# Block-sparse attention and a gated feed-forward layer on one core: half of the head-splitting copies change engine, and the attention stage is ordered anew

## The chip, the core and the metric

The kernel runs on one core of a Trainium2 chip. A core has five engines with instruction queues of their own: PE (TensorE, matmuls and transposes into PSUM; PEld is its loading of weights), DVE (VectorE), ACT (ScalarE), POOL (GpSimd) and SP (SyncE, which here only issues DMAs). Each engine works through its queue in order, and an instruction that waits holds up all that stand behind it on that engine. The metric is the device time of one execution in microseconds (us). Here 1% is 2.1 us.

## The reference

Attention over 4 batches, 8 heads, 768 positions and 64 columns per head, with a mask by blocks of 32 positions: a block sees its neighbours, the first and the last block, and three sampled blocks; the first and the last block see all. The result, as 3072 tokens of 512 columns, goes through a feed-forward layer with 1024 columns inside.

```python
scores = scale * np.matmul(q, k.transpose(0, 1, 3, 2))
mask = |blk_i - blk_j| <= 1, or first or last block in i or j, or kb in sampled_blocks[qb]
scores = np.where(mask, scores, -1e9)
attn = softmax(scores) @ v                 # -> x, (3072, 512)
h = x @ w_in                               # (3072, 1024)
solu = h * softmax(h)
ln = (solu - mean(solu)) / np.sqrt(var(solu) + 1e-6) * g_ln
out = ln @ w_out                           # (3072, 512)
```

## The kernel before, in words

**Layout.** Heads are taken in pairs (`pr`, 0 to 3). For a pair, K and Q are needed with the head's columns on the partitions: `kT` and `qT` hold, per pair, six chunks of 128 positions for each of two heads, on 64 + 24 partitions. The 24 are mask rows, so that one matmul over 88 partitions gives score plus mask; no mask is applied elsewhere. There are two buffers of each, for even and odd batches. `va` holds V with a column of ones, which gives the softmax's sum.

**Batch 0** is transposed by PE: `opening(pr)` casts a staged pair to bf16 (`cast`, L269), turns it on PE into a PSUM bank (`turned`, L463), and copies the bank to `kT` or `qT` (`evac`). The first pair comes in pieces, so that the first scores can begin early: K's first two chunks, then its other four in one piece of eight transposes and one evacuation.

**Batches 1 to 3** are transposed by the DMA crossbar. `crossed(b, pr, nm)` casts a loaded pair to bf16 (`kb`, `qb`), a DMA transposes it (`cross_kq`, issued by SP, into `kc` or `qx`), and there the two heads lie on partitions 0 to 63 and 64 to 127. Two copies named `split` part them: each moves 64 x 768 bf16 values of one head (`hh`) to partitions 0 to 63 of `kT` or `qT`. For `hh` = 1 the source starts at partition 64. There are 3 batches x 4 pairs x 2 tensors x 2 heads = 48 of them.

**Attention** is cut into 3 query tiles `t` of 256 positions. `attend(b, t, pr)` makes three groups of scores (L550, four matmuls each, into one of two PSUM tiles `s`), an exp of each on ACT (L556, 128 x 1024), then 24 matmuls with V (`pv`, L571, into one of two banks `mbank`), a reciprocal and a multiplication (`recip` L580, `norm` L583) into `x`.

**Feed-forward.** For each query tile `x` is transposed (`turn_x`: on PE for the first and the last tile, with `xevac` copies; by DMA otherwise), and each half of 128 tokens (`feed`, j = 0 to 23) runs: x @ w_in (L630, four 512-column matmuls per half of the 1024 columns), exp with sum (`silu_e`, L650, ACT), the product (`mult`, L653, DVE), two `stats` and an `aggr` (L660, L663, DVE), then `z2`, `vr` and `rs` (L666, L669, L702, POOL) for the factor of the row, a transpose of the product, ln @ w_out (L747), `scale` from PSUM to `ots` (L757 on DVE or L755 on ACT) and the store. `scale` frees the `mbank` of its output.

**Weights.** w_in is loaded in four pieces and cast (`wcast`); w_out in two. From w_out and the layer norm's factors VectorE sums rows (`wacc`, L422 and L424) and then makes the eight scaled and centred rows `wo` (L438, two SBUF inputs each); the first output projection needs them.

**Order.** The program is a list of operations. Each call of `op` appends one; `ORDER` gives the order of issue of all of them by their number in that list, and `ENGINES` puts some of them on another engine than the one in their `op` call. What is on one engine runs there in the order of `ORDER`. Buffers come from small pools (`take`, `last_of`), also in that order. A handful of `SPARES`, matmuls whose results nobody reads, stand in the list too.

Of the kernel before, what the change touches and what calls it, by code (L numbers as in the profile page):

```python
# [11 lines left out]
ACT = mybir.ActivationFunctionType  # L12
# [6 lines left out]
    "POOL": [7],  # L19
    "ACT": [9, 24, 127, 383, 543, 811, 1070, 1072, 1114, 1121],  # L20
    "DVE": [90, 92, 126, 134, 135, 154, 411, 622, 639, 653, 657, 863, 867, 872, 876, 886, 1116],
}
ORDER = [
# [112 lines left out]
def kernel(  # L136
# [21 lines left out]
    NPR = H // 2  # L158
# [22 lines left out]
    kT = bufs("kT", [P, NPR, NCH, 2, P], BF16, 2)  # L181
    qT = bufs("qT", [P, NPR, NCH, 2, P], BF16, 2)
# [6 lines left out]
    kc = bufs("kc", [P, NCH, 2, KR], BF16, NKC)  # L189
# [101 lines left out]
    kheld = [own1] + kown[1:]  # L291
# [152 lines left out]
    cover, kdone, qdone, mask1 = [], [], [], {}  # L444
# [409 lines left out]
```

## Time and profile before

| | |
|---|---|
| runs shown | 205.54, 206.61, 206.93 us; median 206.61 |
| profiled execution | 206.22 us, its span 204.2 us |
| granted TensorE clock | 1.000 |
| engines' busy time | PE 197.5, ACT 174.3, DVE 149.4, POOL 66.5 us |
| DMA | 43.17 MB, mean 211 GB/s |

The span runs from the first to the last instruction; 2.0 us lie around it. Lines like "L550" are lines of the kernel. Most copies and casts go through one helper, so they all have line 269 (267 on ACT) and are told apart by what they write and read: `kT<-kc` and `qT<-qx` or `qT<-kc` are the split copies, `kb<-kst` and `qb<-qst` the casts ahead of the crossbar, `va<-vst` V's casts. In a row of groups stand the count, the busy time in us, the mean of one in ns, and the idle time of the engine just before them with what ended it.

### The profile page before, as it was taken

How to read it: one execution, taken by the hardware profiler on the slowest of the kernel's cores; microseconds unless marked ns; L12 is line 12 of the kernel's file. 1: busy time of each engine (PE TensorE's matmuls, PEld its weight loads, DVE VectorE, ACT ScalarE, POOL GpSimd, SP SyncE). 2: the span in 40 equal slices, each digit the busy share in tenths (PEclk: the TensorE clock that was granted, in tenths of full speed). 3: DMA queues.
4: the chain of work that ended last, by engine and by line, in shares of the span. 5: the costliest groups of instructions: out<-in, count | busy, mean ns of one | idle time of the engine just before them, and what ended most of it. 6: DMA issues, size and time to landing. Idle time of an engine off the chain costs nothing.

```text
span 204.2 us, 5675 instructions
## 1 busy us (share of the span) xinstructions
PE 197.5 (97%) x2263; PEld 140.9 (69%) x2292; DVE 149.4 (73%) x332; ACT 174.3 (85%) x219; POOL 66.5 (33%) x141
## 2 busy tenths in 40 slices
PE   8999999989999999999999999999999999999993
PEld 4789887757658768566757777667677586675452
DVE  3478979999979387839976676599929636686772
ACT  4699999989989999999899899979998997784750
POOL 5662465330652234332302514022060110132160
PEclk9999999999999999999999999999999999999999
DMA  5999999999999999979999999999960921327524
GB/s 141 347 369 381 384 377 180 216 244 196 192 253 313 242 249 239 187 182 184 216 206 253 318 204 270 164 210 229 248 203 16 211 48 36 70 102 158 154 84 177
DMA packets 72358, 43.17 MB, mean 211 GB/s; under 512 B 53316, under 2 KB 67148, under 8 KB 72332
## 3 DMA queue, kind: packets, MB, share of 16 engines
q1 hardware_dynamic: 72296, 42.81, 87.5%
q8 instruction: 18, 0.29, 0.6%
q14 instruction: 8, 0.07, 0.1%
q10 hardware_dynamic: 36, 0.00, 0.0%
HBM read 23.07 MB, written 6.29 MB: 144 GB/s over the span
## 4 chain that ended last, share of the span: by engine, by line
PE 90%; DVE 4%; ACT 3%; issue 1%; ACTq 0%
PE s L550 29%; PE mbank L747 19%; PE h L630 17%; PE mbank L571 16%; ACT ex L556 3%; PE h L463 2%; PE h L813 2%; DVE w_out_sb L438 2%; PE mbank L813 1%; PE mbank L770 1%; PE s L630 1%; DVE bs L660 1%; DVE kT L269 1%; PE mbank L463 0%; DVE x L583 0%
## 5 line engine op out<-in xcount | busy, mean ns | idle before, releaser
L556 ACT ACTIVATE ex<-s 128x1024 bf16<-128x1024 f32 x144 | 141.0, 1026 | 15.0 <-PE s L550 13.2
L550 PE MATMUL s<-qT,kT 88*128 88x256 bf16 x576 | 83.1, 272 | 0.5 <-DVE qT L269 0.2
L550 PEld LDWEIGHTS <-kT 88*128 88x128 bf16 x576 | 52.8, 97 | 21.6 <-issue 0.8
L747 PE MATMUL mbank<-w_out_sb,uTs 128*128 128x512 bf16 x173 | 45.6, 379 | 1.2 <-DVE x L583 0.6
L630 PE MATMUL h<-w_in_sb,xT 128*128 128x512 bf16 x167 | 45.4, 379 | 0.8
L571 PEld LDWEIGHTS <-ex 128*128 128x128 bf16 x1152 | 40.9, 97 | 3.5 <-issue 0.2
L571 PE MATMUL mbank<-va,ex 128*128 128x65 bf16 x1152 | 42.2, 194 | 0.1
L653 DVE TENSOR_TENSOR us<-h,e 128x1024 bf16<-128x1024 f32 x22 | 26.8, 1220 | 7.0 <-ACT e L650 6.7
L660 DVE BATCH_NORM_STATS2 bs<-us 128x6 f32<-128x512 bf16 x44 | 28.7, 679 | 0.2
L630 PEld LDWEIGHTS <-xT 128*128 128x128 bf16 x192 | 18.5, 97 | 14.1 <-DMA xT<-x 0.2
L747 PEld LDWEIGHTS <-uTs 128*128 128x128 bf16 x184 | 17.3, 97 | 13.9 <-issue 0.8
L669 POOL TENSOR_SCALAR vr<-z,mv 128x1 f32<-128x1 f32 x22 | 6.6, 298 | 60.1 <-DVE mv L663 52.4
L580 DVE RECIPROCAL r<-mbank 128x4 f32<-128x4 f32 x48 | 8.2, 173 | 24.1 <-PE mbank L571 20.5
L650 ACT ACTIVATE e<-h 128x1024 bf16<-128x1024 f32 x22 | 22.6, 1026 | 1.3 <-POOL vr L669 1.3
L757 DVE TENSOR_SCALAR ots<-mbank,rs 128x512 f32<-128x512 f32 x20 | 14.9, 746 | 8.4 <-issue 4.3
L583 DVE TENSOR_TENSOR x<-mbank,r 128x256 bf16<-128x256 f32 x48 | 20.1, 420 | 1.1
L702 POOL TENSOR_TENSOR rs<-vr,neg_half 128x1 f32<-128x1 f32 x24 | 14.0, 583 | 1.4
L269 POOL CAST va<-vst 128x768 bf16<-128x768 f32 x10 | 9.2, 925 | 12.6 <-DMA vst<-in_v_dram 12.5
L269 POOL CAST kb<-kst 128x768 bf16<-128x768 f32 x10 | 8.4, 840 | 11.2 <-DMA kst<-in_k_dram 11.2
L666 POOL TENSOR_TENSOR z<-z 128x1 f32<-128x1 f32 x22 | 4.6, 207 | 21.8 <-ACT e L650 21.7
L269 POOL CAST qb<-qst 128x768 bf16<-128x768 f32 x9 | 8.2, 915 | 10.3 <-DMA qst<-in_q_dram 10.3
L269 DVE COPY kT<-kc 64x768 bf16<-64x768 bf16 x24 | 10.6, 443 | 0.6 <-DMA kc<-kb 0.2
(112 smaller groups left out, 133.7 us busy)
## 6 DMA issues: line engine op xcount, KB each, us to landing
vst<-in_v_dram SPq DMA_DIRECT2D x16, 384.0 KB, 4.3
out_dram<-ots SPq DMA_DIRECT2D x23, 256.0 KB, 2.7
kst<-in_k_dram SPq DMA_DIRECT2D x15, 384.0 KB, 6.2
qst<-in_q_dram SPq DMA_DIRECT2D x12, 384.0 KB, 5.5
w_out_f<-in_moe_w_out_dram SPq DMA_DIRECT2D x2, 1024.0 KB, 12.6
qst<-in_q_dram SPq DMA_DIRECT2D x4, 256.0 KB, 6.4
uTs<-in_moe_w_in_dram SPq DMA_DIRECT2D x2, 512.0 KB, 11.1
ots<-in_moe_w_in_dram SPq DMA_DIRECT2D x2, 512.0 KB, 10.2
```

What stands on the lines that cost most here:

```text
L269: (nc.vector if o.eng == "DVE" else nc.gpsimd).tensor_copy(out=dst, in_=src)
L550: nc.tensor.matmul(s[:, m, :], kT[i][0:KR, pr, jc, hh, :], qT[i][0:KR, pr, 2 * t : 2 * t + 2, hh, :], start=(m % 2 == 0), stop=(m % 2 == 1))
L556: exs.append(op("exp", "ACT", lambda o, so=so: nc.scalar.activation(out=exb[o.slot], in_=lay["s"][so.slot], func=ACT.Exp, scale=scale), [s ...
L571: nc.tensor.matmul(acc(o)[:, qt, hh, :], exb[exs[n].slot][:, m, qt * P : (qt + 1) * P], va[i][:, 2 * pr + hh, jc, :], start=first, stop=(n ...
L583: nrm = op("norm", "DVE", lambda o: nc.vector.tensor_tensor(out=xb[x_of[b, t].slot][:, :, 2 * pr * D : (2 * pr + 2) * D].rearrange("p a (h ...
L630: nc.tensor.matmul(hx(n), xTb[xt[0].slot][:, qt, c, :], w_in_sb[n][:, c, :], start=(c == 0), stop=(c == KD - 1))
L650: zs = op("silu_e", "ACT", lambda o: nc.scalar.activation(out=eb[o.slots["e"]], in_=lay["h"][0].rearrange("p a f -> p (a f)"), func=ACT.Ex ...
L653: us = op("mult", "DVE", lambda o: nc.vector.tensor_mul(out=ub[o.slot], in0=lay["h"][0].rearrange("p a f -> p (a f)"), in1=eb[zs.slots["e" ...
L660: bs.append(op("stats", "DVE", lambda o, n=n: nc.vector.bn_stats(out=bsb[(bs[0] if bs else o).slot][:, n, :], in_=ub[us.slot][:, w(o, n)]) ...
L702: rs = op("rs", "POOL", lambda o: nc.gpsimd.tensor_tensor(out=rsb[o.slot], in0=vrb[vr.slot], in1=neg_half, op=ALU.pow), [vr, c2], take="rs ...
L747: nc.tensor.matmul(mbank[m0.slot], uTb[ut[0].slot][:, KF // 2 * n + f, :], w_out_sb[n][:, f, :], start=(n == 0 and f == 0), stop=(n == 1 a ...
L757: nc.vector.tensor_scalar(out=otb[o.slot], in0=mbank[os_[0].slot], scalar1=rsb[rs.slot], scalar2=None, op0=ALU.mult)
```

## The change

Three parts.

- `ENGINES`: 26 of the 48 split copies go from VectorE to GpSimd: twelve in batch 1 (all four of pair 0, three of pair 1, all of pair 2, one of pair 3), ten in batch 2, four in batch 3. Fifteen casts go from GpSimd to VectorE (of batch 0: K of pair 1, V of pairs 1 and 2, a Q rest, two w_in pieces; nine of batches 1 to 3), four go the other way. ACT gets two small mask copies, one evacuation of x in the first tile and three output scalings, and gives up the first pair's K cast and evacuation and two scalings; the two halves of the last tile's scaling change places.
- `opening(0)`: the other four chunks of the first pair's K are turned and evacuated in two pieces of two chunks, in two PSUM banks.
- `ORDER`: another order up to the scores of batch 2's last pair in the first query tile; behind that it is the same. All operations from the new one on have numbers higher by two.

On SP, the loads of batch 0's last K, Q and V pairs now stand ahead of all loads of w_in and w_out. On PE, the matmuls are the same; a 256-column spare moves from the opening to the middle of the run.

```diff
 ENGINES = {
-    "POOL": [7],
-    "ACT": [9, 24, 127, 383, 543, 811, 1070, 1072, 1114, 1121],
-    "DVE": [90, 92, 126, 134, 135, 154, 411, 622, 639, 653, 657, 863, 867, 872, 876, 886, 1116],
+    "POOL": [7, 389, 390, 393, 394, 398, 399, 402, 407, 408, 411, 412, 421, 626, 627, 631, 635, 636, 645, 648,
+        649, 657, 658, 863, 864, 873, 876],
+    "ACT": [9, 24, 27, 28, 293, 354, 385, 622, 828, 1072, 1074, 1116, 1120],
+    "DVE": [90, 92, 93, 95, 126, 127, 131, 135, 136, 137, 138, 145, 154, 156, 167, 395, 404, 413, 414, 624,
+        633, 637, 641, 642, 869, 870, 878, 896, 1118],
 }
 ORDER = [
...
             ga = turned(pr, 0, kc, ck, 0, 0, 2, kT[0], [ck] + kown, "ACT", [ck])
-            gb = turned(pr, 0, kc, ck, 2, 2, 6, kT[0], [cr], "DVE", [ck] + kheld)
-            ready_k[0, pr] = [[ga], [gb], [gb]]
+            gb = turned(pr, 0, kc, ck, 2, 2, 4, kT[0], [cr], "DVE", [ck] + kheld)
+            gc = turned(pr, 1, kc, ck, 4, 4, 6, kT[0], [cr], "ACT", [ck] + kheld)
+            ready_k[0, pr] = [[ga], [gb], [gc]]
             ready_q[0, 0, pr] = [gq, mq0]
             cover.append(gq)
-            kdone.extend([ga, gb])
+            kdone.extend([ga, gb, gc])
...
-            for nm, t, done in (("k", kT, kdone[:2]), ("q", qT, [qdone[0], qdone[NPR], mq0])):
+            for nm, t, done in (("k", kT, kdone[:3]), ("q", qT, [qdone[0], qdone[NPR], mq0])):
```

108 rows, old and new, of the table ORDER are left out of this document.

## The prediction

> **What bounds the kernel now.** I read the page first: engine sums and the chain that ended last.
>
> ```profile
> span 204.2 us, 5675 instructions
> PE 197.5 (97%) x2263; PEld 140.9 (69%) x2292; DVE 149.4 (73%) x332; ACT 174.3 (85%) x219; POOL 66.5 (33%) x141
> PE 90%; DVE 4%; ACT 3%; issue 1%; ACTq 0%
> ```
>
> PE is busy 97% and carries 90% of the chain, so the end is set by how long PE's fixed work takes plus the holes in it. A busy PE is not a full PE, so I priced its work from the chain in order of time, where pieces run back to back (start, length, what):
>
> ```profile
> 5.89 0.47 PE h L463 x4
> ...
> 10.03 0.45 PE h L463 x8
> ...
> 46.63 0.73 PE mbank L571 x24
> 47.36 0.88 PE s L550 x8
> ...
> 53.78 0.86 PE mbank L747 x4
> ...
> 60.30 0.86 PE h L630 x4
> ...
> 199.85 1.05 PE mbank L770 x8
> 200.97 0.47 ACT ots L778
> ```
>
> A score matmul costs 0.88/8 = 0.110 us, a probability-times-V matmul 0.73/24 = 0.030, a 512-column one of the feed-forward part 0.86/4 = 0.215, a transpose 0.45/8 = 0.056. The page's groups give the counts (weight loads, because some matmul records are missing):
>
> ```profile
> L550 PEld LDWEIGHTS <-kT 88*128 88x128 bf16 x576 | 52.8, 97 | 21.6 <-issue 0.8
> L571 PEld LDWEIGHTS <-ex 128*128 128x128 bf16 x1152 | 40.9, 97 | 3.5 <-issue 0.2
> L630 PEld LDWEIGHTS <-xT 128*128 128x128 bf16 x192 | 18.5, 97 | 14.1 <-DMA xT<-x 0.2
> L747 PEld LDWEIGHTS <-uTs 128*128 128x128 bf16 x184 | 17.3, 97 | 13.9 <-issue 0.8
> ```
>
> 576 x 0.110 = 63.4, 1152 x 0.0304 = 35.0, 192 x 0.215 = 41.3, 184 x 0.215 = 39.6; the code's 136 transposes add 7.6 and the last 16 matmuls some 1.9. That is 188.8 us. From 5.89 to the end of the last piece at 200.90 are 195.0 us. **So 6.2 us of holes and filler is all that any reordering could win** between the first transposes and the end, and the stretch before 5.89 waits for the first loads. Next: where are the holes?
>
> ```profile
> core 0: us, PE busy (x) PEld busy (x) DVE busy (x) ACT busy (x) POOL busy (x), PEclk, DMA share, GB/s
> 8.00:20.00 12.00, 11.94 (x173) 10.67 (x173) 8.76 (x23) 11.42 (x13) 6.46 (x10) 1.00 1.06 373
> 20.00:34.00 14.00, 13.77 (x210) 11.39 (x209) 12.46 (x28) 13.63 (x15) 7.75 (x10) 1.00 1.09 339
> 34.00:48.00 14.00, 13.20 (x171) 9.90 (x172) 13.79 (x27) 12.95 (x18) 4.19 (x6) 1.00 1.01 210
> 48.00:62.00 14.00, 13.89 (x128) 9.13 (x128) 12.72 (x29) 13.11 (x15) 6.57 (x13) 1.00 1.05 226
> 62.00:110.00 48.00, 47.51 (x563) 34.01 (x567) 34.89 (x78) 44.80 (x54) 14.36 (x26) 1.00 1.08 222
> 110.00:200.00 90.00, 89.12 (x988) 61.20 (x1003) 63.77 (x142) 74.36 (x103) 22.48 (x58) 1.00 0.71 166
> ```
>
> Three limits follow one another. From 8 to 34 ACT is full (11.42 of 12, 13.63 of 14: one softmax exp after the other). From 34 to 48 VectorE is (13.79 of 14), and PE has its only large deficit (13.20 of 14). After 48 PE is, to the end. The place in the middle, seen on PE and on ACT:
>
> ```profile
> 42.91 1.02 PE L747 MATMUL mbank<-w_out_sb,uTs 128*128 128x512 bf16 x4 [0.64 <-DVE x L583]
> ```
>
> ```profile
> 44.40 1.02 ACT L556 ACTIVATE ex<-s 128x1024 bf16<-128x1024 f32 x1 [0.60 <-PE s L550]
> 45.80 1.02 ACT L556 ACTIVATE ex<-s 128x1024 bf16<-128x1024 f32 x1 [0.38 <-PE s L550]
> ```
>
> PE stood 0.64 us at the first output projection (L747), and ACT then missed two scores, 0.98 us in all.
>
> **The change part by part.** *Copies to GpSimd.* 26 of the 48 `split` copies leave VectorE. Casts and the nearest GpSimd copy by form, then kT's split copies by tile (ns min/median/max):
>
> ```profile
> L269 DVE CAST va<-vst 128x768 bf16<-128x768 f32 x6 | 3.8, 634 | 0.0
> L269 POOL CAST kb<-kst 128x768 bf16<-128x768 f32 x10 | 8.4, 840 | 11.2 <-DMA kst<-in_k_dram 11.2
> L269 POOL COPY kc<-kc 128x144 bf16<-128x144 bf16 x1 | 0.4, 366 | 0.1
> ```
>
> ```profile
> L269 DVE COPY kT<-kc x24: 325/354/993, 41.6 to 143.3; 64x768 bf16<-64x768 bf16 x24
> ```
>
> VectorE gets back 26 x 0.354 = 9.2 us (Q's copies are of the same size). In return fifteen casts go from GpSimd to VectorE and four the other way: some 11 x 0.6 = 6.6 back on. The trace has no 64x768 bf16 copy on GpSimd, nor one that shifts 64 partitions (14 of the 26 do, hh=1). Nearest: the cast of 768 f32 elements, 0.84, and a bf16 copy of 144, 0.366. The copy moves half the bytes per element and is no cheaper than the line between would have it, so I let time go by elements. I take 0.84. Ends: 0.35 (VectorE's own median) and 1.7 (two passes of 0.84, if the shift costs one). At 0.84 GpSimd gains 22 us and gives up some 10, from 66.5 to 78 of 204: room enough overall, not everywhere.
>
> *VectorE, 34 to 48.* In this stretch lie the first feed-forward tiles and the eight scaled w_out rows (L438) that PE's first output projection needs. Four copies leave it, and two bn_stats are ordered behind it. What they cost, and what the two engines cost each other, stands in VectorE's and GpSimd's rows in order of time:
>
> ```profile
> 37.03 2.01 DVE L438 SCALAR_TENSOR_TENSOR w_out_sb<-w_out_f,g_sb,wbar 128x512 bf16<-128x512 f32 x2
> ...
> 39.57 0.73 DVE L438 SCALAR_TENSOR_TENSOR w_out_sb<-w_out_f,g_sb,wbar 128x512 bf16<-128x512 f32 x1
> 40.23 0.68 DVE L660 BATCH_NORM_STATS2 bs<-us 128x6 f32<-128x512 bf16 x1
> ...
> 41.58 0.88 DVE L269 COPY kT<-kc 64x768 bf16<-64x768 bf16 x1
> ...
> 42.78 0.34 DVE L269 COPY qT<-qx 64x768 bf16<-64x768 bf16 x1
> ```
>
> ```profile
> 34.76 0.19 POOL L666 TENSOR_TENSOR z<-z 128x1 f32<-128x1 f32 x1 [1.95 <-ACT e L650]
> ...
> 37.67 0.83 POOL L269 CAST kb<-kst 128x768 bf16<-128x768 f32 x1 [0.96 <-DMA kst<-in_k_dram]
> 40.93 1.32 POOL L269 CAST qb<-qst 128x768 bf16<-128x768 f32 x1 [2.43 <-DMA qst<-in_q_dram]
> ...
> 51.04 0.33 POOL L669 TENSOR_SCALAR vr<-z,mv 128x1 f32<-128x1 f32 x1 [8.53 <-DVE mv L663]
> ...
> 53.12 0.56 POOL L702 TENSOR_TENSOR rs<-vr,neg_half 128x1 f32<-128x1 f32 x1
> ```
>
> The copies take 0.88 + 0.34 + 2 x 0.35 = 1.9, the two bn_stats 2 x 0.68 = 1.4: 3.3 us less. Against that: beside a GpSimd cast, two L438 rows took 2.01 instead of 1.46, and a copy 0.88 instead of 0.35: about 0.55 per meeting. With three or four such meetings VectorE is still 1 us ahead, which covers PE's 0.64 and most of the 0.98. Next late is ACT, which has no time to spare. I take **-1.0** (ends -1.6 and 0).
>
> *ACT.* It receives one x evacuation, two small mask copies and three output scalings; two scalings leave, and a cast and an evacuation before its first exp. Only what lies between 8 and 34 is on the path: 0.4 for the x evacuation (an estimate: a quarter of the columns of an exp that takes 1.02, and a fixed part) and less for one mask copy; one exp that now stands behind the first `silu_e` relieves that point. **+0.4** (0 to +0.7).
>
> *First pair's K rest.* One evacuation becomes two of half the width. Both end on VectorE, since the table puts the second there too. The first exp waits for the first K piece and Q, not for this, and the third score group comes when ACT is already full: **0**, covered by the exps (-0.2 to +0.3).
>
> *Loads on SP.* The four w_in and two w_out loads move behind the last K, Q and V loads of batch 0. In 8 to 34 the DMA engines are full (share 1.06 to 1.09, 339 to 373 GB/s), so the sum of bytes sets when the last weight lands, and the last w_out load keeps its place: **0**. K of pair 1 and 2 of batch 1 is crossed earlier, which only helps.
>
> *GpSimd's queue.* In order, it holds up what stands behind a wait. Behind `vr` of tile 0, which waited 8.53 us for VectorE's aggregate, now stand `rs` and the two Q copies of batch 1's pair 2, then `vr`/`rs` of tiles 1 and 2, which free PSUM banks through `scale`. I follow it. The aggregate came at 51.0; 1.4 us of bn_stats now stand ahead of it, less the 1.0 gained: 51.4. `vr` and `rs` add 0.33 + 0.56, two copies 1.7: 54.0. PE took that pair's first scores here:
>
> ```profile
> 57.09 0.60 PE L550 MATMUL s<-qT,kT 88*128 88x256 bf16 x4
> ```
>
> In the new order 1.4 us less of PE's work stands ahead of them, and by the gain above they are 1.0 sooner: 54.7. It just holds. **+0.3** (0 to +2).
>
> *Filler.* One 256-column spare moves from the opening into the stream: **+0.1**.
>
> Sum: -1.0 + 0.4 + 0 + 0 + 0.3 + 0.1 = -0.2 on the profiled execution's 206.2 (span 204.2 and 2.0 around it), so 206.0. On the median of the three times, 206.6, the same sum gives 206.4; I keep **206.0**.
>
> **The rivals.** *A, slower: the GpSimd copy is dear.* Place: 34.8 to 54.7, where eleven copies must end in time for batch 1's first three pairs. Of these 19.9 us, five casts take 4.2, `z`, `vr` and `rs` about 1.7 (an estimate from their rows of 0.19, 0.33 and 0.56), and a late load 2.4 (the wait at 40.93). That leaves 11.6, so it decides at 11.6/11 = 1.05 us a copy. At 1.4, between that and the end of 1.7, the queue is 0.35 x 11 = 3.9 us late and PE waits: **209.9**; at 1.7, 213. For it: the shift is not in the trace. Against: both GpSimd rows fit one price by elements.
>
> *B, slower: the two engines get in each other's way.* Eleven copies in the stretch 34 to 56, each meeting a VectorE instruction for 0.55, cost 6.1 against 3.3 won, and VectorE, full there, hands 2.8 to PE: **209.0**. For it: the max of 993 beside the median of 354. Against: the median itself, most copies met nobody. The Trainium skill, "SBUF — State Buffer", section "Who interferes with whom", states it as a rule: VectorE in a two-port mode, or with two SBUF inputs against a reading GpSimd instruction, and GpSimd exclude one another for a whole instruction. By that rule, at its worst, all 26 copies hold VectorE up for their full length, and the gain above is gone; by it the time would be at least B's. The trace agrees on the mechanism (0.88 beside 0.35) and not on the worst case.
>
> *C, faster: the holes close.* Besides the 1.0 in the middle, half of what is left of the 6.2 (2.6) goes, because VectorE, lighter, feeds the opening sooner: 206.2 - 3.6 = **202.6**; with a quarter (1.3) 203.9. Against: ACT is full there and gets more to do.
>
> **How the numbers follow.** A measurement of this kernel tells about 1% (2 us) from no change. Forecast, within 1%: 0.41, own range 204.6 to 207.9. A 0.20, B 0.16, C 0.23. A and B lie over 1% slower, C over 1% faster: 0.23, 0.41, 0.36. The range leaves out a third of C and half of A, 0.18 in all: 203.2 to 210.8.
>
> **What would show it.** GpSimd's kT and qT copies with a mean near 0.84 (A: over 1.1). No PE gap at the first L747 after 40, no ACT gap of 0.6 there. VectorE below 13 of 14 in 34 to 48 (B: full, and L438 over 1.0 on average). No PE wait for qT from GpSimd near 54. PE's work from 62 on unchanged: a difference that arises after 62 would make me wrong about the place. I am wrong on the sum if the opening's exps shift by more than 1 us either way.

## The result and the profile after

The changed kernel takes 207.38 us (median of 16 runs, 206.52 to 209.16) beside 206.53 us of the kernel before on the same chips. The ratio is **1.0048, 95% interval 1.0029 to 1.0066**: 1.0 us slower. The forecast was 206.0, 0.2 us below its execution of before. One count in the description of the change, and in the prediction, is wrong: fourteen casts go from GpSimd to VectorE and five the other way, not fifteen and four. That is nine casts net instead of eleven; no term of the sum rests on it.

Behind `opening(0)` the lines of the changed kernel stand two or three further down: the score is L553, the pv matmul L574, the norm L586, the output projection L750, the scaled w_out row L440, the helper of copies and casts L271. Its page, the rows that answer to those shown of before:

```profile
span 206.2 us, 5694 instructions
...
PE 197.3 (96%) x2262; PEld 140.4 (68%) x2292; DVE 148.6 (72%) x314; ACT 174.1 (84%) x221; POOL 80.8 (39%) x158
...
PE 67%; DMA 17%; POOL 6%; issue 3%; DVE 3%; SPq 1%; POOLq 0%; DVEq 0%
...
L271 POOL COPY kT<-kc 64x768 bf16<-64x768 bf16 x14 | 12.1, 862 | 3.7 <-DMA kc<-kb 3.2
...
L440 DVE SCALAR_TENSOR_TENSOR w_out_sb<-w_out_f,g_sb,wbar 128x512 bf16<-128x512 f32 x8 | 7.9, 1031 | 0.1
```

GpSimd has 14 us more to do, and VectorE, which gave up 26 copies, has 0.8 us less. PE's share of the chain fell from 90% to 67%: GpSimd (6%) and DMA transfers (17%) now stand in it. Much of this fall belongs to one execution: in a second profile of the same kernel, below, PE has 82%, GpSimd 1% and DMA transfers 3%. The copy costs what was predicted, 0.862 us on average. The scaled w_out row costs 1.031 us; in the kernel before its min, median and max were 726, 744 and 1354 ns. The same stretches as before (PE, PEld, VectorE, ACT and GpSimd busy; clock; DMA share; GB/s):

```profile
8.00:20.00 12.00, 11.19 (x162) 9.79 (x163) 8.53 (x22) 10.79 (x13) 3.04 (x6) 1.00 0.98 319
20.00:34.00 14.00, 13.65 (x198) 11.48 (x199) 12.32 (x31) 13.78 (x16) 5.40 (x7) 1.00 1.05 385
34.00:48.00 14.00, 13.14 (x177) 9.69 (x176) 13.48 (x21) 12.96 (x18) 9.76 (x10) 1.00 1.13 173
48.00:62.00 14.00, 13.65 (x120) 8.74 (x119) 12.45 (x23) 12.27 (x16) 10.37 (x19) 1.00 1.10 222
62.00:110.00 48.00, 47.67 (x561) 34.13 (x566) 34.40 (x71) 45.29 (x54) 21.11 (x36) 1.00 1.04 238
110.00:200.00 90.00, 88.55 (x1003) 61.04 (x1018) 62.30 (x134) 75.90 (x105) 25.16 (x60) 1.00 0.72 160
```

Between 34 and 62 GpSimd has 20.1 of 28 us busy where it had 10.8, and VectorE still 13.48 of 14 in the stretch where it was to be relieved. PE did not gain in the middle (13.14 after 13.20), and lost in 48 to 62, in 8 to 20 and behind 110. PE's waits in the middle, in order of time, and then ACT's:

```profile
42.96 0.89 PE L574 MATMUL mbank<-va,ex 128*128 128x65 bf16 x24 [0.31 <-DVE x L586]
...
47.22 0.60 PE L553 MATMUL s<-qT,kT 88*128 88x256 bf16 x4 [0.32 <-POOL qT L271]
...
56.97 0.60 PE L553 MATMUL s<-qT,kT 88*128 88x256 bf16 x4 [0.24 <-POOL qT L271]
```

```profile
44.33 1.94 ACT L559 ACTIVATE ex<-s 128x1024 bf16<-128x1024 f32 x2 [1.00 <-PE s L553]
```

The 0.64 us in front of the first output projection are gone. In their place PE waits for a norm one instruction later, and ACT misses the same 1.0 us that it missed before. Then come two waits that the kernel before did not have, both for a Q copy on GpSimd. GpSimd's rows around them:

```profile
40.49 1.33 POOL L271 CAST qb<-qst 128x768 bf16<-128x768 f32 x1
41.77 1.28 POOL L271 CAST kb<-kst 128x768 bf16<-128x768 f32 x1
...
45.89 1.28 POOL L271 COPY qT<-qx 64x768 bf16<-64x768 bf16 x1
...
54.24 0.27 POOL L672 TENSOR_SCALAR vr<-z,mv 128x1 f32<-128x1 f32 x1 [1.22 <-DVE mv L666]
...
55.22 1.70 POOL L271 COPY qT<-qx 64x768 bf16<-64x768 bf16 x2
```

Pair 0's Q copy ends at 47.17 and the matmul starts at 47.22; pair 2's two end at 56.92 and the matmul starts at 56.97. The second is the queue that the prediction followed, with its wait for the aggregate (`vr`, 1.22); the first it did not look at.

### The profile page after: what moved, and what is told of

It reads as the page before. It is cut to its first block, busy times and chain, and to the rows that moved or that the text cites. A ratio compares the mean times of both kernels' runs of the same rounds, so it can differ in the third digit from the quotient of the medians.

```text
span 206.2 us, 5694 instructions
## 1 busy us (share of the span) xinstructions
PE 197.3 (96%) x2262; PEld 140.4 (68%) x2292; DVE 148.6 (72%) x314; ACT 174.1 (84%) x221; POOL 80.8 (39%) x158
## 4 chain that ended last, share of the span: by engine, by line
PE 67%; DMA 17%; POOL 6%; issue 3%; DVE 3%; SPq 1%; POOLq 0%; DVEq 0%
PE s L553 21%; PE mbank L750 16%; PE h L633 15%; PE mbank L574 13%; DMA qst<-in_q_dram 9%; DMA us<-in_q_dram 3%; DMA kst<-in_k_dram 3%; DMA qx<-qb 2%; POOL qT L271 2%; SPq L354 1%; POOL qb L271 1%; POOL kT L271 1%; PE mbank L773 1%; DVE bs L663 1%; PE s L633 1%
## 5 line engine op out<-in xcount | busy, mean ns | idle before, releaser
L553 PE MATMUL s<-qT,kT 88*128 88x256 bf16 x576 | 82.9, 272 | 0.9 <-POOL qT L271 0.6
L553 PEld LDWEIGHTS <-kT 88*128 88x128 bf16 x576 | 52.8, 97 | 22.5 <-issue 1.9
L750 PE MATMUL mbank<-w_out_sb,uTs 128*128 128x512 bf16 x170 | 45.2, 379 | 0.7
L574 PEld LDWEIGHTS <-ex 128*128 128x128 bf16 x1152 | 40.8, 97 | 4.9 <-issue 1.1
L574 PE MATMUL mbank<-va,ex 128*128 128x65 bf16 x1152 | 42.2, 193 | 1.0 <-DVE x L586 0.7
L750 PEld LDWEIGHTS <-uTs 128*128 128x128 bf16 x184 | 17.3, 97 | 13.1
L586 DVE TENSOR_TENSOR x<-mbank,r 128x256 bf16<-128x256 f32 x48 | 20.2, 420 | 1.2
L760 DVE TENSOR_SCALAR ots<-mbank,rs 128x512 f32<-128x512 f32 x19 | 14.2, 746 | 9.5 <-PE mbank L750 3.1
L705 POOL TENSOR_TENSOR rs<-vr,neg_half 128x1 f32<-128x1 f32 x24 | 13.5, 560 | 1.5
L271 POOL COPY kT<-kc 64x768 bf16<-64x768 bf16 x14 | 12.1, 862 | 3.7 <-DMA kc<-kb 3.2
L271 POOL CAST qb<-qst 128x768 bf16<-128x768 f32 x11 | 10.3, 940 | 3.0 <-DMA qst<-in_q_dram 1.5
L271 POOL CAST kb<-kst 128x768 bf16<-128x768 f32 x7 | 6.4, 916 | 7.1 <-DMA kst<-in_k_dram 7.0
L440 DVE SCALAR_TENSOR_TENSOR w_out_sb<-w_out_f,g_sb,wbar 128x512 bf16<-128x512 f32 x8 | 7.9, 1031 | 0.1
```

What stands on the lines that cost most here:

```text
L271: (nc.vector if o.eng == "DVE" else nc.gpsimd).tensor_copy(out=dst, in_=src)
L553: nc.tensor.matmul(s[:, m, :], kT[i][0:KR, pr, jc, hh, :], qT[i][0:KR, pr, 2 * t : 2 * t + 2, hh, :], start=(m % 2 == 0), stop=(m % 2 == 1))
L574: nc.tensor.matmul(acc(o)[:, qt, hh, :], exb[exs[n].slot][:, m, qt * P : (qt + 1) * P], va[i][:, 2 * pr + hh, jc, :], start=first, stop=(n ...
L586: nrm = op("norm", "DVE", lambda o: nc.vector.tensor_tensor(out=xb[x_of[b, t].slot][:, :, 2 * pr * D : (2 * pr + 2) * D].rearrange("p a (h ...
L705: rs = op("rs", "POOL", lambda o: nc.gpsimd.tensor_tensor(out=rsb[o.slot], in0=vrb[vr.slot], in1=neg_half, op=ALU.pow), [vr, c2], take="rs ...
L750: nc.tensor.matmul(mbank[m0.slot], uTb[ut[0].slot][:, KF // 2 * n + f, :], w_out_sb[n][:, f, :], start=(n == 0 and f == 0), stop=(n == 1 a ...
```

## A second profile of the changed kernel

The first profile has two more places: transposes in the opening that wait 0.69 us for Q chunks, and this one behind 110 (PE, then VectorE):

```profile
116.27 0.90 PE L574 MATMUL mbank<-va,ex 128*128 128x65 bf16 x24 [0.41 <-DVE x L586]
```

```profile
114.66 1.00 DVE L271 CAST kb<-kst 128x768 bf16<-128x768 f32 x1 [1.73 <-DMA kst<-in_k_dram]
```

Nothing in the prediction stands for either. Before they are explained, the changed kernel is run and profiled once more without an edit, on the same chip as its variants.

> The changed kernel, nothing altered, for a second profile of it on the same chip as its variants. Theory NOISE (two places of the first profile are of that one execution): the transposes of pair 1's Q come at 8.9 to 9.2 in place of 9.9, the 0.8 us gap near 116 is under 0.4, and PE stands 0.9 us behind the column sums near 35 as in the run with one cast back. If they are of the kernel, both come again at 0.9. Ratio 1.003 to 1.0065 either way.

Measured: 1.0050 (1.0021 to 1.0078), the same ratio as before. **The opening's wait did not come again; the gap near 115 did, smaller (0.27 us).** The opening's is one slow load of that execution. The load of these chunks, in the DMA view of the first and of the second profile (the last number is us from issue to landing):

```profile
us<-in_q_dram SPq DMA_DIRECT2D x1, 384.0 KB, 7.2
```

```profile
us<-in_q_dram SPq DMA_DIRECT2D x1, 384.0 KB, 6.0
```

6.0 is also what it took in the kernel before. So 0.7 us at the start of the first profile are chance, and they can hide what was late behind them. In the second profile PE's two largest waits are

```profile
35.58 0.38 PE L435 MATMUL mbank<-ex,onesf 128*128 128x512 bf16 x1 [0.83 <-DVE x L586]
...
43.24 0.89 PE L574 MATMUL mbank<-va,ex 128*128 128x65 bf16 x24 [0.60 <-DVE x L586]
```

The first is the column sums of w_out (`cs`), a wait that the profile of the kernel before does not have. The waits for GpSimd differ as well: pair 0's Q copy ends at 44.97, and PE does not wait for it; pair 2's two end at 56.63, and PE waits 0.15 us where it waited 0.24.

## The experiments

**The loads put back.** The first 22 loads on SP in the order of before:

```diff
-    k02 behind g; K of pair 3 ahead of V of pairs 2 and 3; w_in, w_out behind all of them
+    g behind k02; V of pair 2, K of pair 3, w_in#91, w_out#101, ..., V of pair 3, w_in#85, w_in#94, w_out#102
```

> The changed kernel, with its first 22 loads on SP in the order of before (g behind K of pair 2, V of pair 2 ahead of K of pair 3, the first w_in and w_out loads between them); all else as changed. Theory LOADS (the opening's 0.9 us come from the order of the loads: the first Q chunks of pairs 1 to 3 land 1.1 us later): the transposes that wait for them go back from 10.35 to about 9.4, PE's work between 13 and 34 stands within 0.2 us of before's, and the ratio to before falls from 1.0048 to about 1.001. Rival ABSORBED (ACT and VectorE are full behind it, so that an earlier start is lost again by 34): the transposes move, the ratio stays at 1.004 to 1.006. Rival NOISE (the late landing is of that one profiled execution): the transposes stand at 9.4 to 10.4 whatever the order, the ratio stays.

Measured: **1.0111** (1.0092 to 1.0131), 1.3 us slower still than the changed kernel. All three theories fall. The opening's transposes were early, and then PE stood at 24.4 (in this run's file the transposes are L476 and the helper L282):

```profile
24.42 0.25 PE L476 MATMUL mbank<-ident,qr 128*88 128x128 bf16 x1 [1.20 <-POOL qr L282]
```

The new order of the work needs the new order of the loads, though not for Q's sake. On GpSimd the cast of this Q rest (`qr`, at 23.75) stands behind a cast of w_in that waited 7.02 us for its load and started at 23.19; in the changed kernel that wait is 4.21 us, and the w_in cast starts at 21.23. It is an in-order queue again. Putting the loads back does not win the 1.0 us.

**The copies back on VectorE, and the copies alone.**

```diff
 ENGINES = {
-    "POOL": [7, 389, 390, 393, 394, 398, 399, 402, 407, 408, 411, 412, 421, ...],
+    "POOL": [7],
```

> The changed kernel with its 26 copies back on VectorE, at the same places of the order. Theory COPIES (the move to GpSimd itself costs, by its 0.84 us a copy and by meetings with VectorE): the ratio to before falls below 1.002 and the scores of batch 1's pair 2 no longer wait for GpSimd near 56. Theory PLACES (the order costs in three places, the move pays in the middle): VectorE, which has 13.48 of 14 us busy from 34 to 48 with the copies away, gets 11 x 0.35 = 3.9 us back on between 39 and 57 and passes 1 to 3 us of it to PE; the ratio is 1.008 to 1.018.

Measured: **1.0690** (1.0653 to 1.0727), 14 us slower. More than any theory said, and for another reason. One row on VectorE tells it (here the helper is L281):

```profile
38.12 0.35 DVE L281 COPY kT<-kc 64x768 bf16<-64x768 bf16 x1 [11.92 <-DMA kc<-kb]
```

The new order has batch 1's first K copy far ahead of its data. On VectorE every norm stands behind it: VectorE stood for 11.9 us, PE for 10.75 (at 39.07), ACT for 11.58. This run says that order and engines belong together. It says nothing on the price of a copy. The other way round, before's order with only these 26 copies on GpSimd:

> The kernel before with nothing changed but the 26 copies, which run on GpSimd at the places of the old order. Theory PLACES (the copies pay where VectorE is full, if they do not stand behind long waits): the 0.64 us that PE stands at the first output projection near 43 go, but the copies of pair 1 and 2 come behind casts and behind the wait for the aggregate near 51, with 0.6 to 1.3 us of slack at before's; ratio 0.998 to 1.010. Theory COPIES: every copy that meets VectorE costs, the ratio is above 1.005 and the rows of the scaled weights (L438) take more than 1.0 us on average in place of 0.82.

Measured: 1.0037 (1.0013 to 1.0061), within the range of PLACES; the scaled rows took 0.94 us on average, where COPIES asked for over 1.0. PE's rows (here score L562, output projection L759, helper L281):

```profile
42.94 1.03 PE L759 MATMUL mbank<-w_out_sb,uTs 128*128 128x512 bf16 x4
...
48.63 1.02 PE L759 MATMUL mbank<-w_out_sb,uTs 128*128 128x512 bf16 x4 [0.45 <-DVE w_out_sb L450]
...
58.35 0.49 PE L562 MATMUL s<-qT,kT 88*128 88x256 bf16 x3 [0.44 <-POOL qT L281]
...
63.69 0.50 PE L562 MATMUL s<-qT,kT 88*128 88x256 bf16 x3 [0.65 <-DVE kT L281]
```

The hole at the first output projection is closed: this much of the prediction's -1.0 is real, and the copies alone do it. Then it is given back: first to a scaled row on VectorE (the four rows ahead of 48.6 took 4.31 us, in the kernel before 2.73), then to a copy on GpSimd, then to one on VectorE. **That is the whole change in small: a gain near 42, paid back between 46 and 64.**

**The cast.** The gap near 115 stands behind one cast that went to VectorE.

```diff
-    "DVE": [..., 869, 870, 878, ...],
+    "DVE": [..., 869, 878, ...],
```

> The changed kernel with one cast (K of batch 3's pair 1) back on GpSimd, where it was before. In the changed kernel it stands on VectorE at 114.66 after a wait of 1.73 us for its load, ahead of the reciprocal and the multiplication that PE waits for. Theory CAST: the reciprocal of that pair goes back from 115.6 to about 113, PE's gap of 0.8 near 116 goes, and the ratio to before falls from 1.0048 to about 1.001. Rival LOAD (what is late is the load, and something else waits for it): the gap moves on to the copies of that pair or to ACT, and the ratio stays at 1.004 to 1.006.

Measured: 1.0062 (1.0035 to 1.0088), no better. In this run's own profile the gap near 115 is gone and the reciprocal comes at 112.45 instead of 115.59, as CAST had it; the time did not follow. The same edit on top of others, `e12_all` below, has the gap again: with the cast on GpSimd, V's cast behind it is late, and PE waits there.

```profile
114.61 0.89 PE L574 MATMUL mbank<-va,ex 128*128 128x65 bf16 x24 [0.48 <-POOL va L271]
```

By the ratio LOAD holds rather than CAST: these runs show no time that moving this cast would win.

**The weights, the queue, and both.** First the edits meant for the column sums:

```diff
 ENGINES
-    "DVE": [90, 92, 93, 95, ...]
+    "DVE": [90, 92, ...]
 ORDER
+    93, 95 ahead of 387 (batch 1's first K cast)
-    52 (load of K, batch 1, pair 2) behind 49
+    52 behind 388 (the first crossbar DMA)
```

> The changed kernel with two edits that let the row sums of w_out (wacc) end sooner: the two w_in casts that went to VectorE run on GpSimd again, ahead of batch 1's first K cast, and the load of K of batch 1's pair 2 stands behind the first crossbar DMA again, as before, so that its 384 KB do not share the DMA engines with the last w_out load. Theory WEIGHTS (the last of these rows ends at 34.8 to 35.0 in place of 34.1, and PE stands 0.9 us behind the column sums near 35, where the opening was in time): the first of VectorE's second four rows starts at 30.5 to 31.0 in place of 31.5 to 31.7, the last ends by 34.2, the gap behind the column sums falls from 0.93 to under 0.3, and the ratio falls by 0.003 to 0.004, to 1.001 to 1.003. Rival QUEUE (what costs are the Q copies on GpSimd, at 46.5 and 56.4): PE is early by that much at 40 and waits the longer at 46.5; the ratio stays at 1.004 to 1.006.

Then three copies off GpSimd's queue, or earlier in it:

```diff
 ENGINES
-    "POOL": [..., 411, 412, ...]
+    "DVE": [..., 411, 412, ...]
 ORDER
-    398, 393
+    393, 398
-    302, 303, 412, 411, 318
+    412, 411 directly ahead of 308 (the first scale, on VectorE)
```

> The changed kernel with three copies placed otherwise: on GpSimd the Q copy of batch 1's pair 0 (head 0) stands one place earlier, ahead of a K copy of pair 1, and the two Q copies of pair 2 run on VectorE, directly ahead of the scaling that waits 0.7 us for GpSimd's factor there. Theory QUEUE: PE's gaps of 0.58 behind the first scores of batch 1 (46.5) and of 0.51 behind the first scores of pair 2 (56.4) go, and the ratio falls by 0.004 to 0.005, to about 1.000. Rival ACT (the exps behind these scores are late anyway, because ACT had lost its time at 35): the gaps move by less than 3 us along the run, and the ratio stays above 1.003.

> Both sets of edits together. If WEIGHTS and QUEUE each name a cost of its own, they add: 0.9 + 1.0 = 1.9 us below the changed kernel, ratio 0.994 to 0.998, faster than both kernels. If only one of them is a real cost, the ratio equals that of the run with that set alone. If what is won before 62 is given back later, it stays above 1.002.

Measured: weights 1.0018 (0.9994 to 1.0042); **queue 1.0000 (0.9978 to 1.0022)**; both 1.0023 (0.9993 to 1.0052). The changed kernel, run on the same chip, stands at 1.0050: the queue's edits are worth all that separates it from the kernel before, 1.0 us, as their theory said. With the copies of pair 2 on VectorE PE no longer waits near 56; at 46.6 a wait of 0.32 is left.

Where the 1.0 us are won, this pair of profiles shows only in part. Ahead of pair 2's scores PE's rows are 0.37 us apart (an output projection at 55.49 in the second profile of the changed kernel, at 55.12 here), behind them 0.69 (the scores at 56.67 and 55.98). So 0.32 us are won at these Q copies. The rest of the 0.8 us between the two executions lies at the column sums, the norm near 43 and the gap near 115.

The weights' edits seem to win too, but not by their theory: the second four rows started at 31.62, not at 30.5 to 31.0, and PE still waited 0.43 us for the column sums. GpSimd's rows of that run:

```profile
44.07 0.82 POOL L271 COPY qT<-qx 64x768 bf16<-64x768 bf16 x1
...
54.05 1.70 POOL L271 COPY qT<-qx 64x768 bf16<-64x768 bf16 x2
```

Pair 0's Q copy ends at 44.9 and pair 2's at 55.8, and PE waits for neither. Beside the first profile of the changed kernel that is 2.3 and 1.2 us earlier, but beside the second only 0.1 and 0.9: most of it is a difference between executions. What the weights' edits win, if anything, is not shown. Nor is it shown why the two sets do not add; that both cure the same cost is one reading. In `e7_both` PE has a longer wait at the norm. PE and VectorE:

```profile
42.75 0.89 PE L574 MATMUL mbank<-va,ex 128*128 128x65 bf16 x24 [1.01 <-DVE x L586]
```

```profile
35.95 1.25 DVE L440 SCALAR_TENSOR_TENSOR w_out_sb<-w_out_f,g_sb,wbar 128x512 bf16<-128x512 f32 x1
...
37.45 2.20 DVE L440 SCALAR_TENSOR_TENSOR w_out_sb<-w_out_f,g_sb,wbar 128x512 bf16<-128x512 f32 x2
...
40.18 1.97 DVE L440 SCALAR_TENSOR_TENSOR w_out_sb<-w_out_f,g_sb,wbar 128x512 bf16<-128x512 f32 x2
```

Five scaled rows took 5.42 us instead of 5 x 0.74 = 3.70 (5.02 in the second profile of the changed kernel), with GpSimd's copies and casts beside them; PE waited 1.0 us for the norm behind them.

**The row.** The fifth scaled row stands ahead of that norm without need. It goes behind the second norm:

```diff
-    118, 121, 257, 258, 313, 275, 276, 122
+    118, 257, 258, 313, 275, 276, 121, 122
```

> The changed kernel with that one row moved and nothing else. Theory MEETINGS: the hole of 0.65 to 0.95 us at 42.3 goes, but the Q copies on GpSimd still hold PE at 46.5 and 56.4, so that part of it is waited for there; the ratio falls from 1.005 to 1.001 to 1.003. Rival QUEUE ALONE (GpSimd's queue sets the scores at 46.5 whatever comes before): ratio 1.004 to 1.006.

> The run with the three copies placed otherwise, and one of the eight scaled w_out rows moved on VectorE: the fifth stands behind the two multiplications (norm) of batch 0's last tile at 42 to 44, with the other three, where it stood ahead of the first. The second output projection needs it only near 48. Theory MEETINGS (near 42 PE waits for a norm that stands behind this row, and the row takes 1.30 us in place of 0.74 because GpSimd casts and copies beside it): the hole near 42 (0.29 in that run) is under 0.1, and the ratio falls from 1.000 to 0.997 to 0.999. Rival PE-FULL (the hole is made good later by PE anyway): the ratio stays at 1.000.

> Both sets of edits and the same row moved. Theory MEETINGS (the two sets did not add, 1.0023, because the K that loads and crosses earlier brings four GpSimd copies and casts beside the scaled rows between 36 and 42, which put the norm off and open PE's hole of 1.35 us at 41.4): the hole falls below 0.4, and the ratio to 0.995 to 0.998. Rival NOT-ADDITIVE (PE and ACT have no room for more): the hole moves on to 46 or 56, and the ratio stays at 1.001 to 1.004.

> As the run before the last (both sets and the row), and the cast of K of batch 3's pair 1 back on GpSimd. Theory CAST (in the second profile of the changed kernel PE's gap near 115 came again, 0.68 us, and it is absent where the cast is on GpSimd): the gap goes and the ratio is 0.001 to 0.003 below that of both sets and the row, 0.993 to 0.997. Rival LOAD: no difference between the two, within 0.001.

Measured: row alone 1.0057 (1.0030 to 1.0084); with the queue's edits 1.0021 (0.9996 to 1.0046); with both sets 1.0006 (0.9977 to 1.0036); and with the cast 1.0008 (0.9985 to 1.0030). In none of the four does the profile mark a wait of PE for a norm near 42. The row alone and the row with the queue's edits differ in the same three copies as the changed kernel and `e6_queue`, on another chip: 0.0036 here, 0.0050 there. With the row alone PE waits for the Q copies, 0.79 us at 46.9 and then

```profile
57.25 0.60 PE L553 MATMUL s<-qT,kT 88*128 88x256 bf16 x4 [0.90 <-POOL qT L271]
```

That is QUEUE ALONE: **in this execution GpSimd sets the pace between 46 and 57, and what is won ahead of it is waited for.** How long PE waits there varies. With these three copies as in the change, its waits for Q copies on GpSimd between 46 and 58, as the profile marks them in brackets, come to 0.56 and 0.15 us in the two profiles of the changed kernel, 0.60 in `e4_cast`, 0.17 in `e1_loads`, 0 in `e5_wout` and 1.69 here; with the queue relieved to 0.32 in `e6_queue` and to none in `e7_both`, `e9_queue_row`, `e10_both_row` and `e12_all`. With the queue relieved, MEETINGS' hole closes, but the ratios, 1.0006 to 1.0021, do not fall to the 0.995 to 0.999 that it asked for.

**The meeting of the two engines.** The rows leave out the subtraction of the mean row and read one operand from SBUF:

```diff
-    nc.vector.scalar_tensor_tensor(out=..., in0=w_out_f..., scalar=g..., in1=wbar, op0=mult, op1=subtract)
+    nc.vector.tensor_scalar(out=..., in0=w_out_f..., scalar1=g..., scalar2=None, op0=mult)
```

> The changed kernel, in which the eight scaled w_out rows leave out the subtraction of the mean row, so that each reads one operand from SBUF in place of two (VectorE's work is less by that). Theory TWO INPUTS (a row that reads two operands from SBUF and a GpSimd copy or cast keep each other waiting, 0.74 to 1.3 us for the row and 0.82 to 1.3 us for the copy): the rows take the same time whether GpSimd copies or not, and the GpSimd copies and casts beside them stay at 0.82 to 0.85. Rival ANY COPY MODE (every VectorE instruction with all operands in SBUF meets GpSimd so): the rows still spread by a factor of 1.5 or more, and copies of 1.1 to 1.3 us stay between 37 and 47.

A single run took 205.72 us, beside a median of 206.40 of before on that chip; its time is not drawn on. VectorE's rows by tile (ns, min/median/max), then GpSimd's of that stretch:

```profile
L440 DVE TENSOR_SCALAR w_out_sb<-w_out_f,g_sb x8: 456/478/1042, 36.3 to 44.7; 128x512 bf16<-128x512 f32 x8
```

```profile
39.70 1.05 POOL L271 CAST kb<-kst 128x768 bf16<-128x768 f32 x1
...
41.66 1.70 POOL L271 COPY kT<-kc 64x768 bf16<-64x768 bf16 x2
```

Neither theory holds whole. GpSimd's rows fall to 0.82 to 1.05, yet three of the eight VectorE rows still took about twice their 0.47. So a row with one operand and all of it in SBUF meets GpSimd too. What does not meet it at all is the bn_stats, 44 of them before and after (by tile), though in the changed kernel two run at 52.0 and 52.6 beside a GpSimd copy (52.21 to 53.03):

```profile
L660 DVE BATCH_NORM_STATS2 bs<-us x44: 640/679/696, 36.1 to 190.4; 128x6 f32<-128x512 bf16 x44
```

```profile
L663 DVE BATCH_NORM_STATS2 bs<-us x44: 639/681/696, 51.3 to 192.3; 128x6 f32<-128x512 bf16 x44
```

The Trainium skill, "SBUF — State Buffer", section "Who interferes with whom", says which instructions meet: VectorE's with two SBUF inputs beside a GpSimd instruction that reads SBUF, and one-input copies, casts and scalings in their two-port modes; others with one input do not. The trace agrees on who meets: rows with two inputs go from 0.74 to 1.30 us, scalings from 0.47 to 1.04, bn_stats stay at 0.70 or less. In which mode the scalings ran, no run shows. The section calls it an exclusive lock: in the two-port modes, whoever issues first has the shared ports for the whole instruction, and the other blocks. Between a row and a copy back to back such a lock would make both 0.74 + 0.82 = 1.56 us long (an estimate from these rows by the page's rule); most that met took 1.2 to 1.35, about 0.5 us more on either side.

**Six copies, in the old order.**

```diff
 ENGINES
+    "POOL": [..., 387, 388, 391, 392, 643, 647]
 ORDER
+    387, 394, 391, 398, 392, 388, 403, 407
```

> The kernel before in its own order, with six copies on GpSimd in place of 26: the four of batch 1's pair 0, with the casts of pair 1 between them, and two K and Q copies of batch 2's pair 2, ahead of a cast that waits for its load. Theory ROOM (the copies pay only where VectorE holds PE up and GpSimd is idle: PE's two holes of before, 0.70 at 42.0 and 0.44 at 94.3): both holes fall under 0.2, nothing waits behind GpSimd, and the ratio to before is 0.994 to 0.997, faster than both kernels. Rival MEETINGS (each copy beside a scaled w_out row stretches it from 0.74 to 1.3 us, and VectorE gives the gain back): the hole at 42 stays over 0.4 and the ratio is 0.999 to 1.003.

Measured: 0.9991 (0.9969 to 1.0012), MEETINGS' figure. PE at the first output projection, and VectorE ahead of it:

```profile
43.48 0.81 PE L747 MATMUL mbank<-w_out_sb,uTs 128*128 128x512 bf16 x3 [0.70 <-DVE x L583]
```

```profile
37.52 2.84 DVE L438 SCALAR_TENSOR_TENSOR w_out_sb<-w_out_f,g_sb,wbar 128x512 bf16<-128x512 f32 x2
```

Two rows took 2.84 us instead of 1.49, beside two copies and two casts; the second alone took 2.08. Each copy that leaves VectorE gives back 0.35 us, and a meeting takes 0.5 or more.

**The order without GpSimd.** Two bn_stats moved, nothing else; then the Q copy for which PE stood at 94; then the bn_stats moved further back:

```diff
-    296 ahead of 238 (norm), 297 behind 115
+    296, 297 behind 265 (norm, 48.1)
```

```diff
-    642, 564, 643, 647, 637, 509, 634, 646
+    642, 646, 564, 643, 647, 637, 509, 634
```

```diff
-    296, 297 behind 265; 298 behind 397
+    296, 297, 298 behind 283 (norm, 51.4); 300, 331 behind 412 on GpSimd
```

> The kernel before with one piece of the new order alone, and no copy on GpSimd: the two bn_stats of the first feed-forward half, which VectorE ran at 36.1 and 40.2 ahead of the scaled w_out rows, stand behind the norm at 48.1. Theory ORDER (what relieves VectorE between 34 and 48 in the changed kernel is this move, 1.35 us, and not the copies): PE's hole of 0.70 at the first output projection near 42 falls under 0.3, GpSimd's copies cost nothing because there are none, and the ratio to before is 0.996 to 0.999. Rival SHIFTED (the 1.35 us are late behind 48, where VectorE is as full): PE waits at 48 to 54 instead, ratio 0.999 to 1.002.

> As the run before, and one more move on VectorE without GpSimd: the Q copy of batch 2's pair 2 (head 0) for which PE stood 0.44 us at 94.3 stands directly behind that pair's first K copy, where VectorE was idle for 1.06 us. Theory ORDER: both holes of before go, together some 1.0 us; ratio 0.994 to 0.997, faster than both kernels. Rival SHIFTED: what is won is waited for at the next place, ratio 0.999 to 1.002.

> The kernel before with every copy on VectorE, the Q copy of batch 2's pair 2 moved as in the run before, and the two bn_stats with their aggregate one stage further back: behind pair 1's four copies and the norm at 51.4, ahead of the other tiles' bn_stats; on GpSimd the factor's first step (vr) and one small sum (z2) stand behind the cast of pair 3's K. In the run with the bn_stats at 48, the hole at 42 was closed and 0.9 us were lost again at 50.8, where PE waited for pair 1's K and Q copies behind them. Theory PLACE (that wait is the only price of the move): no hole at 42, none at 51, none at 94, and 0.8 + 0.4 us are kept; ratio 0.993 to 0.997, faster than both kernels. Rival SHIFTED (VectorE is full up to 57, so that the 1.35 us of work make something else late wherever they stand): a new wait between 52 and 62, ratio 0.998 to 1.001.

Measured: 1.0005 (0.9979 to 1.0032), 0.9987 (0.9965 to 1.0010), 1.0004 (0.9987 to 1.0020). PE in the first of them:

```profile
42.28 1.03 PE L747 MATMUL mbank<-w_out_sb,uTs 128*128 128x512 bf16 x4
...
51.71 0.92 PE L550 MATMUL s<-qT,kT 88*128 88x256 bf16 x7 [0.41 <-DVE qT L269]
```

No wait at 42: **the move of two bn_stats, 1.35 us, closes the hole by itself, with every copy on VectorE.** And it is waited for at 51.7 behind pair 1's copies. In the third run both waits are gone, and its profile marks no wait of PE over 0.3 us between 14 and 62; the time is the same. A new one stands there all the same, unmarked. PE comes to an output projection at 57.25 (57.53 in the kernel before) and, behind a pv group that starts at 60.72 and takes 0.73, to the next scores at 61.74 (61.73): 0.29 us later than it could, just behind a K copy of VectorE that ends at 61.68. The lead is gone there. SHIFTED holds for the first and the third run; the second, 0.9987, lies between the ranges of the two theories.

**The last w_out load one place earlier.**

```diff
-    88, 101, 91, 85, 94, 102
+    88, 101, 91, 85, 102, 94
```

> The run with the three copies placed otherwise and the row moved, and on SP the last w_out load one place earlier, ahead of the last w_in load. Theory WEIGHTS (what makes PE wait behind the column sums near 35, 0.3 to 0.8 us in every variant of the new order and nothing before, is the landing of the last w_out load at about 31.4, which all small loads ahead of it put off): VectorE's second four rows start at 30.4 to 31.0, the gap behind the column sums falls under 0.2, and the ratio falls by 0.001 to 0.003 below 1.002. Rival ROWS (VectorE reaches these rows no earlier whatever has landed, because of four casts of w_in and two multiplications ahead of them): they start at 31.2 to 31.7 as before, the gap stays at 0.3 to 0.8.

Measured: 1.0029 (0.9999 to 1.0058), no better than the 1.0021 without it. The time alone does not tell WEIGHTS from ROWS, and its rows are not drawn on; the question stays open.

## Why the prediction was wrong, by its own steps

- **GpSimd's queue, +0.3 (0 to +2): this is the step that failed, by its size.** The place was named and "It just holds" was the reading; it does not. I had pair 2's Q copies end at 54.0, 0.7 us ahead of PE. They end at 56.92 and 56.63 in the two profiles, and PE waits for them. The copies cost what I said: from the start of `vr` to their end are 2.68 us, and I had 0.33 + 0.56 + 1.7 = 2.6. Late is the aggregate ahead of them: `vr` starts at 54.24 and 53.95, where I had 51.4. VectorE's rows of the first profile:

```profile
51.34 0.69 DVE L663 BATCH_NORM_STATS2 bs<-us 128x6 f32<-128x512 bf16 x1
51.95 0.17 DVE L583 RECIPROCAL r<-mbank 128x4 f32<-128x4 f32 x1
52.03 1.25 DVE L663 BATCH_NORM_STATS2 bs<-us 128x6 f32<-128x512 bf16 x2
53.20 0.41 DVE L586 TENSOR_TENSOR x<-mbank,r 128x256 bf16<-128x256 f32 x1
53.52 0.20 DVE L666 BATCH_NORM_AGGREGATE mv<-bs 128x2 f32<-128x12 f32 x1
```

  Three bn_stats, a reciprocal and a norm stand ahead of the aggregate. I had counted two bn_stats, 1.4 us, and had taken off 1.0 us for a gain that VectorE did not make. Pair 0's Q copy I did not look at; it ended at 47.17 in the first profile and held PE up, and at 44.97 in the second and did not. Beside the casts and copies that I priced at 0.84 stand five of about 1.28 between 40 and 48 in the first profile. By the runs the queue costs 1.0 us: three copies off it or earlier in it are worth 0.0050, and 0.0036 in the second pair.
- **VectorE, -1.0:** the mechanism is right, the size is not, and it was put to the copies' credit. VectorE stayed at 13.48 (I had said below 13). PE no longer waits at the first output projection, but it waits for the norm behind the stretched rows instead, and ACT's miss is as before (1.00). I had three or four meetings still leave 1 us of gain; they did not. For the hole at the first output projection two moved bn_stats do as much as 26 copies.
- **ACT +0.4, K's rest 0, filler +0.1:** in the second profile PE has a single wait, of 0.23 us, between 10 and 34. None of the three shows as a loss.
- **Loads on SP, 0:** no loss comes from them, but "the last w_out load keeps its place" is too short. Put back, they cost 1.3 us: a cast of w_in then waits longer for its load, and a Q rest behind it on GpSimd holds PE up for 1.20. Whether "K of pair 1 and 2 is crossed earlier, which only helps" holds stays open: with pair 2's K loaded later and two casts moved, the Q copies ended 0.1 and 0.9 us earlier than in the second profile.
- **Not foreseen: the column sums.** In the kernel before they run without a wait, behind the last row sum (PE, then VectorE):

```profile
34.22 0.60 PE L433 MATMUL mbank<-ex,onesf 128*128 128x512 bf16 x2
```

```profile
33.38 0.75 DVE L424 SCALAR_TENSOR_TENSOR ex<-w_out_f,g_sb,wbar 128x512 bf16<-128x512 f32 x1
```

In the new order they stand behind one more group of pv matmuls, and PE waits 0.24 to 1.15 us there in the second profile and in nine variants (`e1_loads`, `e4_cast`, `e5_wout` to `e7_both`, `e9_queue_row` to `e12_all`). VectorE's rows of the second profile:

```profile
33.63 1.35 DVE L426 SCALAR_TENSOR_TENSOR ex<-w_out_f,g_sb,wbar 128x512 bf16<-128x512 f32 x1
34.90 0.17 DVE L583 RECIPROCAL r<-mbank 128x4 f32<-128x4 f32 x1
35.11 0.42 DVE L586 TENSOR_TENSOR x<-mbank,r 128x256 bf16<-128x256 f32 x1
```

The norm ends at 35.53 and the column sums start at 35.58; the profile puts PE's wait down to this norm, which stands behind the last row sum. That row took 1.35 us where it took 0.75 in the kernel before. My reading is that the bank that the column sums take is the one that this norm frees; that is argued, no run has taken it away.
- **The rivals:** A falls (0.862, not over 1.05). B is right that the two engines stretch each other and wrong in its price: I had VectorE hand 2.8 us to PE. VectorE's part is the norm near 43 (0.31 and 0.60 us) and the late aggregate, and the whole change is 1.0 us slower. C falls. "A difference that arises after 62" does exist (0.27 us at 115), but it is small and moving its cast did not lower the time.
- **The sum:** the queue is +1.0 instead of +0.3, and all the rest together is 0 (with the queue relieved the ratio is 1.0000) where I had -0.5: the gain near 42 is small instead of -1.0 (0.31 to 0.60 us are waited for there where it was 0.64). The column sums' 0.2 to 1.2 are in that rest. The measured 207.4 lies inside the range of 204.6 to 207.9 by the width of the range alone: the forecast was faster, the kernel is slower.

What stays open: what the wait for the column sums costs by itself, and by which path the three copies are worth 1.0 us when PE's marked waits for them come to 0 to 1.7 us in one execution or another. Of the kernel before there is a single profile, so its small waits, too, are those of one execution. In no run was a version faster than the kernel before beyond its interval; the nearest are 0.9987 (0.9965 to 1.0010) and 0.9991.

## What to carry to other kernels

Where an engine is full and another idle, price a move on both queues: the idle engine's in-order queue, with everything that it waits for on the way, decides when the result is there. Look for the order first: two independent instructions out of the way closed the same hole here as 26 copies on another engine, and neither made the kernel faster. And profile the same kernel twice before explaining a wait under one us: one of the two extra places in the first profile was a single slow load, and an edit that seemed to bring a copy 2.3 us earlier had brought it 0.1 us earlier than the second profile.

## What the runs showed of the hardware

- A GpSimd copy of 64 x 768 bf16 takes 0.82 us whether its source starts at partition 0 or 64, and as long as a cast from f32 of 768 elements on 128 partitions; VectorE's takes 0.35.
- Copies and casts on GpSimd and two-operand rows on VectorE stretch each other, 0.82 to 1.28 and 0.74 to 1.30 in most meetings, once to 2.08; bn_stats of one bf16 operand are not touched (696 ns at most, in both kernels).
- The landing of one early 384 KB load varied from 6.0 to 7.2 us between two executions of one kernel, which shifted PE's work at 10 us by 0.7 us.
